# A RetNet block and a quick-GELU MLP on one core: a new order of loads, conversions and products up to the fifth unit

## The chip, the cores and the metric

The kernel runs on one core of one Trainium2 chip, as one launch. A core has five engines that work side by side, each through its own queue of instructions in order: PE (TensorE, matrix products; PEld is its loading of stationary operands), DVE (VectorE, elementwise), ACT (ScalarE, elementwise functions and copies), POOL (GpSimd, elementwise) and SP (SyncE, which here only issues DMAs). DMAs are issued by SP, ACT and POOL. The metric is the device time of one execution in microseconds (us), the median over runs.

## The reference, cut to what matters

Two parts, one after the other. `retnet_recurrent` keeps a 64 x 64 state for each of 4 batches and 8 heads over 768 positions:

```python
for t in range(S):                          # S = 768
    state = gamma[h] * state + outer(k[:, :, t], v[:, :, t])
    y[:, :, t] = scale * q[:, :, t] @ state
```

Its output, put together over the heads, is `x` with 3072 rows of 512. `act_gelu_quick` then computes

```python
h = x @ w_in                                # 512 -> 2048
g = h * (1 / (1 + exp(-1.702 * h)))
out = g @ w_out                             # 2048 -> 512
```

All inputs are float32 for q, k, v and 64-bit floats for `w_in` and `w_out`, which the kernel gets as pairs of 32-bit words and narrows itself to float32. The result is float32.

## The kernel before, in words

**Units.** The recurrence is done in chunks of 64 positions. A unit j is one chunk for two batches (batch on the two halves of the 128 partitions) and all eight heads. Units 0 to 11 are the first two batches. For a unit:

- `load(j)` fetches q (SP, four DMAs of 64 KB for j < 6), k (POOL, for unit 0 ACT, four DMAs) and v (SP, two DMAs of 128 KB). q and v have two buffers each, so unit j+2 loads into the buffer of unit j once that is done with.
- `turn(j)` transposes q and k on PE for j < 6: four 128 x 128 transposes each, into two PSUM tiles; `turned(j)` copies them to SBUF on ACT. From unit 6 on, the transposes are done on DVE (L253).
- `step{j}-{f}` is `attend(j, f)` on PE: for unit j the products k by q (L289, PSUM tile `pa`), and for an earlier unit f its state update k by v (L297), its share from the state (L306) and from the chunk itself (L312, PSUM tile `py`). `step{j}` is the first part alone, `step-{f}` the others alone. `pa` and `py` have one buffer each.
- `masked(j)` on DVE multiplies `pa` by a causal decay mask (L318). `decay(j)` on ACT scales k by its decay (L272, eight instructions). `aged(f)` on ACT scales the state (L357), `updated(f)` on DVE adds the new part (L366 for unit 0, a copy, and L368). `state{f}` (L325) and `x{f}` (L347, for unit 0 a copy on ACT, L349) on DVE put the output of the unit into X.

**Weights.** The weights come in sixteen pieces: w0 to w7 of `w_in`, w8 to w15 of `w_out`, each as two DMAs of 512 KB on SP ("a" and "b", L180) into one of three raw buffers (piece number modulo 3). Piece 0 is converted by halves, the others whole. A conversion is one ACT instruction, `abs` (L207), and six on DVE: `half` (L211, L212, L213) and `rest` (L217, L218, L222). A raw buffer is free for its next piece when `rest` is done.

**Products.** `up0.th.p` (L414, 16 matmul instructions of 256 columns) is the first MLP product for two units (th = 0: units 0 and 1, th = 1: units 2 and 3) with weight piece p; `gate` applies quick-GELU on ACT (L393). The first blocks of products are begun as soon as their units and weight pieces are there, between the steps of later units; from unit 8 on, the kernel runs in a regular order that this change does not touch.

**Start.** The mask is made from `rows` (a product on PE, L862), `mask` (DVE, L901) and `causal` (two instructions on POOL, L866). `rowd` (ACT, L872) reads `rows` too; `whole` (POOL, two small DMAs) loads the state's decay. `warm` is a matmul on PE whose result nobody reads. `table` loads ACT's function table.

**The order.** What each engine does until the regular part starts is written out by hand as one list of names, and carried out name by name. `pin` keeps an instruction in that order on its engine, and PE is wholly in program order. The relative order of two names matters only where they use the same engine or the same buffer. The change rewrites the first seven lines of that list.

Of the kernel before, what the change touches and what calls it, by code (L numbers as in the profile page):

```python
# [9 lines left out]
F32 = mybir.dt.float32  # L10
U32 = mybir.dt.uint32
AF = mybir.ActivationFunctionType
# [16 lines left out]
def kernel(  # L29
# [29 lines left out]
    pe, act, dve, pool, sp = nc.tensor, nc.scalar, nc.vector, nc.gpsimd, nc.sync  # L59
# [41 lines left out]
    rowd = const.tile([P, HP, D], F32, name="rowd")  # L101
# [3 lines left out]
    whole = const.tile([P, HP], F32, name="whole")  # L105
    whole_h = const.tile([P, H], F32, name="whole_h")
    ident = const.tile([P, P], F32, name="ident")
    mask = const.tile([P, 2, HP, D], F32, name="mask")
# [9 lines left out]
    def pin(i):  # L118
        return tc.keep_in_program_order(i) if ordered[0] else i
# [62 lines left out]
    class Narrow:  # L182
# [30 lines left out]
            pin(dve.scalar_tensor_tensor(hi, hi, 0x80000000, mu, op0=ALU.bitwise_and, op1=ALU.bitwise_or))  # L213

        def rest(self):
            m, mu, lo, hi = self.m, self.mu, self.lo, self.hi
            pin(dve.tensor_scalar(mu, hi, 0xFF800000, None, op0=ALU.bitwise_and))  # L217
            pin(dve.scalar_tensor_tensor(lo.bitcast(F32), lo, 2.0 ** -52, m, op0=ALU.mult, op1=ALU.mult))  # L218
            a, b = lo.bitcast(F32), hi.bitcast(F32)
            if self.i < NFF:  # L220
                a, b = [t.rearrange("p (c ab f) -> p c ab f", ab=2, f=P) for t in (a, b)]
            pin(dve.tensor_add(self.w, b, a))  # L222
# [8 lines left out]
    def home(j, name):  # L231

        at = ["qT", "kT", "kd", "at"].index(name)
        shape = [[HP, P] if j < NEW else [H, D]] * 2 + [[H, D], [2, HP, D]]
        shape = shape[at]
        if j >= 2 * CB:
            return one.tile([P] + shape, F32, name=name, tag=name, bufs=[2, 1, 1, 2][at])
        t = G[:, at, j % 2 * 2:j % 2 * 2 + 2].rearrange("p s t -> p (s t)")
        return t.rearrange("p (a b c) -> p a b c", a=2, b=HP) if at == 3 else t.rearrange("p (a b) -> p a b", a=shape[0])

    def turn(j):

        QT[j], KT[j] = home(j, "qT"), home(j, "kT")
        if j < NEW:

            x = QKV.pop(("q", j)), QKV["kn", j]
            TURNED[j] = p = [ps.tile([P, HP, P], F32, name="pt", tag="y") for i in range(2)]
            for n in (1, 0) if j else (0, 1):
                for s in range(HP):
                    pe.matmul(p[n][:, s, :], x[n][:, 2 * s:2 * s + 2].rearrange("p r d -> p (r d)"), ident, is_transpose=True)  # L250
        else:
            for t, name in ((QT[j], "q"), (KT[j], "k")):
                tc.keep_in_program_order(dve.transpose(  # L253
                    t.rearrange("p h t -> p (h t)"), QKV.pop((name, j)).rearrange("p h n d -> p (h n d)")))
        if 2 * CB <= j < NCH - 2:
            load(j + 2, "qk")

    def turned(j):
        p = TURNED.pop(j)
        for n in (1, 0) if j else (0, 1):  # L260
            pin(act.activation((QT[j], KT[j])[n], p[n], AF.Copy))

    def decay(j):
# [98 lines left out]
    def updated(f):  # L362
        c = f % NC
        new, u = state[(c + 1) % 2], PU.pop(f)
        if c == 0:
            pin(dve.tensor_copy(new, u))  # L366
        elif c < NC - 1:
            pin(dve.tensor_add(new, new, u))  # L368

    def step(j, f=None):  # L370
        attend(j, f)
        if j is not None:
            masked(j)
            if j > 2 * CB:
                decay(j)
        if f is not None:
            c = f % NC
            if c == 0:
                updated(f)
            else:  # L380
                by_state(f)
            output(f)
            if 0 < c < NC - 1:
                aged(f)
                updated(f)
        if j is not None and 2 * CB < j < NCH - 1:
            load(j + 1, "v")
# [255 lines left out]
    def down49(m, ring, comps):  # L643
# [25 lines left out]
        def home2(name, first, rest):  # L669
            kept[name] = first.rearrange("p (j e) -> p j e", e=P), rest[:, 0:3 * P].rearrange("p (j e) -> p j e", e=P)  # L670
            return kept[name]
# [169 lines left out]
    works, products = {}, {}  # L841
# [63 lines left out]
    for j in range(2 * CB):  # L905
        for name in "qkv":
            works[f"{name}{j}"] = lambda j=j, name=name: load(j, name)
        works |= {f"{name}{j}": lambda j=j, do=do: do(j) for name, do in (
            ("turn", turn), ("turned", turned), ("decay", decay), ("masked", masked), ("state", by_state),
            ("x", output), ("aged", aged), ("updated", updated))}  # L910
        for f in (None, *range(2 * CB)):
            works[f"step{j}" + ("" if f is None else f"-{f}")] = lambda j=j, f=f: attend(j, f)
        works[f"step-{j}"] = lambda j=j: attend(None, j)
# [7 lines left out]
        works[f"w{i // 2}{'ab'[i % 2]}"] = lambda i=i: fetch(i)  # L921
    for name, i in [("0a", 0), ("0b", 1)] + [(str(p), 2 * p) for p in range(1, NFF)]:
        n = Narrow(i)
        works |= {"abs" + name: n.start, "half" + name: n.half, "rest" + name: n.rest}

    units = [0]

# [14 lines left out]

    begin()
    for name in """
        k0 table q0 warm turn0 w0b rows warm k1 abs0b q1 turned0 step0 v0 w0a half0b mask k2 turn1 causal rest0b
        masked0 decay0 v1 decay1 abs0a half0a step-0 updated0 turned1 q2 step1 rowd whole w2b turn2 w2a x0 k3
        aged1 masked1 turned2 v2 rest0a abs2 q3 step-1 updated1 state1 decay2 aged2 step2 q4 x1 half2 decay3 w3b
        w3a up0.0.0 masked2 turn3 k4 step-2 v3 q5 rest2 k5 gate0.0.0 turned3 updated2 state2 step3 up0.0.2
        masked3 abs3 half3 x2 rest3 turn4 w1b step-3 aged3 gate0.0.2 turned4 state3 w1a w5b updated3 v5 decay4
        abs1 x3 turn5 half1 up0.0.3 turned5 up0.1.2 step4 aged4 w5a rest1 v4 gate0.0.3 decay5 w6a masked4  # L950
        gate0.1.2 abs5 w6b step5-4 half5 rest5 up0.0.1 updated4 abs6 state4 gate0.0.1 w4b
        up0.1.1 half6 aged5 w4a up0.0.5 rest6 masked5 up0.1.5 gate0.1.1 x4 gate0.0.5 abs4 step-5 w8b w8a
        half4 gate0.1.5 state5 updated5 anew q6 up0.1.6 x5 rest4 gate0.1.6 abs8 v6 decay6 aged6 up0.0.6 w7b w7a half8
        turn6 gate0.0.6 up0.1.0 abs7 seven_4.2 seven_6.2 half7 gate0.1.0 w9b w9a up0.1.4 q7 gate0.1.4 step6 masked6 rest7 up0.0.4 v7
        gate0.0.4 seven_52.2 turn7 up0.1.3 gate0.1.3 step7-6 seven_4.0 masked7 updated6 decay7 aged7 abs9 state6 x6 up0.0.7 rest8 seven_w.0 gate0.0.7
        w11a w11b step-7 state7 x7 seven_x half9 w10b w10a up0.1.7 gate0.1.7
        seven2.0 seven2.1 abs11 rest9 seven2.2 seven_v.0 w12a w12b seven2.3 half11 seven2.4 abs10 seven_4.1 seven_w.1
        seven2.5 rest11 seven2.6 w14b w14a seven0.0 seven0.1 half10 seven0.2 abs12 seven0.3 rest10 w13a w13b seven0.4
        seven_v.1 seven0.5 seven_4.3 half12 seven_w.3 seven0.6 seven1.0 abs14 seven1.1 rest12 w15a w15b seven1.2 seven1.3
        half14 seven1.4 abs13 seven_v.3 seven1.5 updated7 rest14 seven1.6 seven3.0 seven3.1 half13 seven3.2 abs15 seven3.3  # L960
        rest13 seven3.4 seven3.5 late_loads half15 rest15 seven3.6 seven_end
    """.split():
        works[name]()
    ordered[0] = False
    INNER = [(0, 19), (0, 22), (0, 26), (1, 2), (1, 12), (1, 15), (1, 18)]
    for m in range(NB):
        between = []
        if m == 0:
            between = [lambda: None, lambda: None, lambda: turn(2 * CB), lambda: step(2 * CB), lambda: None,
                       lambda: turn(2 * CB + 1)]  # L970
        elif m == 1:
            between = [lambda: (decay(2 * CB), load(2 * CB + 1, "v"))]
            for j in range(2 * CB + 1, 3 * CB + 1):
                between.append(lambda j=j: (step(j, j - 1), j < 3 * CB and turn(j + 1)))
        elif 1 < m < NB - 1:
            last = min((m + 2) * CB, NCH - 1)
            for j in range((m + 1) * CB + 1, last + 1):
                between.append(lambda j=j: (step(j, j - 1), j < last and turn(j + 1)))
            if last == NCH - 1:
                between.append(lambda: step(None, NCH - 1))  # L980
# [77 lines left out]
```

## Time and profile before

| | |
|---|---|
| median of 3 runs | 662.11 us (660.8 to 662.55) |
| the profiled execution: its own time | 662.24 us |
| its span, first to last instruction | 660.5 us |
| PE busy | 642.2 us, 97% of the span |
| DVE busy | 453.9 us, 69% |
| ACT busy | 159.0 us, 24% |
| POOL busy | 198.8 us, 30% |
| DMA | 91.86 MB, mean 139 GB/s |

The profile is one execution taken by the hardware profiler. Its page gives busy shares of engines, the same in 40 slices of the span (a digit is tenths; PEclk is the clock granted to TensorE), the chain of work that ended last, and the costliest groups of instructions by line. The timeline lists instructions in order of time: start, duration, engine, line, operation, operands, and in brackets the idle time before it with what ended that. A line number is that of the kernel as printed above. Instructions that only issue DMAs, wait or branch do not count as busy.

### The profile page before, as it was taken

How to read it: one execution, taken by the hardware profiler on the slowest of the kernel's cores; microseconds unless marked ns; L12 is line 12 of the kernel's file. 1: busy time of each engine (PE TensorE's matmuls, PEld its weight loads, DVE VectorE, ACT ScalarE, POOL GpSimd, SP SyncE). 2: the span in 40 equal slices, each digit the busy share in tenths (PEclk: the TensorE clock that was granted, in tenths of full speed). 3: DMA queues.
4: the chain of work that ended last, by engine and by line, in shares of the span. 5: the costliest groups of instructions: out<-in, count | busy, mean ns of one | idle time of the engine just before them, and what ended most of it. 6: DMA issues, size and time to landing. Idle time of an engine off the chain costs nothing.

```text
span 660.5 us, 15291 instructions
## 1 busy us (share of the span) xinstructions
PE 642.2 (97%) x6390; PEld 580.2 (88%) x6390; DVE 453.9 (69%) x645; ACT 159.0 (24%) x306; POOL 198.8 (30%) x225
## 2 busy tenths in 40 slices
PE   6789999999999999999999999999999999999997
PEld 3778888888788888889999888999888999988997
DVE  3699989999936973556984445995354995254965
ACT  4674233551000000333100233010233110233110
POOL 6400311310379217000536400445600255500000
PEclk9989999999999999999999999999999999999999
DMA  9995549763233556262485832386742252602142
GB/s 176 193 274 173 152 104 241 172 163 60 49 82 135 137 149 153 58 248 96 118 199 134 279 57 97 86 223 135 225 118 97 66 154 104 235 21 96 55 154 96
DMA packets 148149, 91.86 MB, mean 139 GB/s; under 512 B 131600, under 2 KB 134416, under 8 KB 147056
## 3 DMA queue, kind: packets, MB, share of 16 engines
q1 hardware_dynamic: 135856, 45.19, 29.8%
q0 software_dynamic: 9888, 44.46, 20.6%
q10 hardware_dynamic: 2336, 1.25, 0.6%
q8 instruction: 50, 0.82, 0.5%
q14 instruction: 19, 0.16, 0.1%
HBM read 72.89 MB, written 15.47 MB: 134 GB/s over the span
## 4 chain that ended last, share of the span: by engine, by line
PE 89%; DVE 4%; DMA 4%; SPq 1%; issue 1%; ACT 0%; DVEq 0%
PE pq L666 27%; PE px L562 17%; PE pd L799 13%; PE py L562 13%; PE ph L491 7%; PE ph L414 5%; PE pa L289 2%; PE py L312 2%; PE pa L297 2%; PE py L306 2%; DMA W<-in_moe_w_in_dram 1%; DMA W<-in_moe_w_out_dram 1%; DMA q_in<-in_q_dram 1%; PE pt L250 1%; SPq L140 1%
## 5 line engine op out<-in xcount | busy, mean ns | idle before, releaser
L635 POOL DMA_DIRECT2D ring<-W2D x28 | 15.4, 551 | 227.7 <-PE px L562 118.3
L666 PE MATMUL pq<-W,G 128*128 128x128 f32 x672 | 80.2, 276 | 0.0
L666 PEld LDWEIGHTS pq<-W,G 128*128 128x128 f32 x672 | 77.6, 192 | 1.3 <-issue 0.7
L666 PE MATMUL pq<-ring,own 128*128 128x128 f32 x448 | 60.1, 276 | 1.3 <-issue 1.3
L562 PE MATMUL px<-X,W1A 128*128 128x256 f32 x256 | 59.8, 379 | 0.0
L562 PE MATMUL px<-X,W1B 128*128 128x256 f32 x256 | 59.8, 379 | 0.0
L666 PEld LDWEIGHTS pq<-ring,own 128*128 128x128 f32 x448 | 54.5, 192 | 0.4
L562 PEld LDWEIGHTS px<-X,W1B 128*128 128x128 f32 x256 | 48.5, 190 | 6.7
L562 PEld LDWEIGHTS px<-X,W1A 128*128 128x128 f32 x256 | 48.4, 190 | 6.5
L393 ACT ACTIVATE G<-G 128x512 f32<-128x512 f32 x60 | 37.4, 628 | 54.7 <-DVE G L572 33.4
L799 PE MATMUL pd<-W,G 128*128 128x256 f32 x224 | 49.6, 381 | 0.0
L799 PEld LDWEIGHTS pd<-W,G 128*128 128x128 f32 x224 | 42.2, 190 | 5.9
L562 PE MATMUL py<-X,W1A 128*128 128x256 f32 x192 | 45.4, 379 | 0.0
L562 PE MATMUL py<-X,W1B 128*128 128x256 f32 x192 | 45.4, 379 | 0.0
L562 PEld LDWEIGHTS py<-X,W1A 128*128 128x128 f32 x192 | 36.5, 190 | 5.0
L562 PEld LDWEIGHTS py<-X,W1B 128*128 128x128 f32 x192 | 36.5, 190 | 5.0
L580 DVE TENSOR_TENSOR t<-py,u 128x512 f32<-128x512 f32 x16 | 11.1, 692 | 32.3 <-PE py L562 32.3
L569 ACT ACTIVATE p<-px 128x512 f32<-128x512 f32 x16 | 9.6, 597 | 96.0 <-PE px L562 96.0
L414 PE MATMUL ph<-X,W1A 128*128 128x256 f32 x128 | 30.6, 397 | 0.9 <-DVE X L347 0.9
L594 DVE TENSOR_TENSOR G<-G 128x512 f32<-128x512 f32 (+2 forms) x24 | 12.3, 513 | 25.7 <-ACT G L393 25.7
L666 PE MATMUL pq<-ring,G 128*128 128x128 f32 x224 | 29.6, 275 | 0.0
L666 PE MATMUL pq<-W,own 128*128 128x128 f32 x224 | 29.6, 275 | 0.0
(237 smaller groups left out, 1226.0 us busy)
## 6 DMA issues: line engine op xcount, KB each, us to landing
ring<-W2D POOLq DMA_DIRECT2D x28, 768.0 KB, 4.8
W1B<-W1D POOLq DMA_DIRECT2D x6, 1792.0 KB, 9.8
W<-in_moe_w_in_dram SPq DMA_DIRECT2D x12, 512.0 KB, 5.9
W<-in_moe_w_out_dram SPq DMA_DIRECT2D x10, 512.0 KB, 5.8
out_dram<-o POOLq DMA_DIRECT2D x20, 256.0 KB, 3.0
q_sq<-in_q_dram SPq DMA_DIRECT2D x144, 32.0 KB, 2.1
k_sq<-in_k_dram SPq DMA_DIRECT2D x144, 32.0 KB, 2.1
v_in<-in_v_dram SPq DMA_DIRECT2D x72, 64.0 KB, 3.1
```

Source lines behind the costliest of these rows:

```text
L289: pe.matmul(pa[HALF[w], u, 0, s, :], kt[HALF[u], w, s, :], qt[HALF[u], w, s, :], start=True, stop=True)
L297: pe.matmul(pa[HALF[u], w, 1, s, :], kd[HALF[w], HP * u + s, :], vn[HALF[w], HP * u + s, :], start=True, stop=True)
L306: pe.matmul(py[HALF[o], u, 1, 2 * w + s2, :], old[HALF[u], w, 2 * s2 + o, :], qt[HALF[u], w, 2 * s2 + o, :], start=True, stop=True)
L312: pe.matmul(py[HALF[o], w, 0, 2 * u + s2 if f < NEW else 2 * s2 + u, :], vn[HALF[w], HP * u + s, :], a[HALF[w], u, s, :], start=True, stop ...
L393: pin(act.activation(g, h[:, i], AF.Gelu_apprx_sigmoid))
L414: pe.matmul(h[:, ab], w, X[:, 2 * th + c // 2, c % 2, :], start=(ab == 0 and c == 0), stop=(c == 3), skip_group_check=True)
L491: pe.matmul(acc[:, u, :], w, x, start=(start and u == 0 and c == 0), stop=(stop and c == 1), skip_group_check=True)
L562: pe.matmul(acc[:, u, :], t[:, q1 + u, sa, c, :], X[:, sb, c, :], start=(start and u == 0 and c == 0), stop=(stop and c == 1), skip_group_ ...
L594: dve.tensor_sub(q[0][1], q[0][0], q[0][1])
L635: pool.dma_start(c, W2D[i])
L666: pe.matmul(p0[:, j, :], a[:, d], w[:, d], start=(new and j == 0 and d == 0), stop=(d == NP // 2 - 1), skip_group_check=True)
L799: pe.matmul(p0[:, n, :], g1(m, p, sa)[:, n * P:(n + 1) * P], W2[:, sb, p, :], start=(new and p == 0 and n == 0), stop=(last and p == NP - ...
```

## The change

- The order of names up to unit 5 is new. On SP both halves of w0 are now issued first, ahead of q0 and v0; then w2 ahead of q1 and v1; w3 ahead of q2; w1 ahead of v3 and q4; w5 ahead of v4 and q5.
- On POOL, `causal` and `whole` now stand ahead of the loads of k2.
- `rest` is split into `resta` (two instructions) and `restb` (one), which can stand apart; for pieces 2, 3 and 1 other DVE work now stands between them.
- `turn0` transposes k first and then q, as the other units do; `turned0` likewise.
- `updated0`, a copy of the first state out of PSUM, is done on ACT and no longer on DVE.
- `step2` stands behind the first product and not ahead of it; `step3-2` is one step for units 3 and 2. `turn5` and `turned5` stand behind `step4`, and `abs5` behind `turned5`.

```diff
         def rest(self):
+            self.resta()
+            self.restb()
+
+        def resta(self):
             m, mu, lo, hi = self.m, self.mu, self.lo, self.hi
             pin(dve.tensor_scalar(mu, hi, 0xFF800000, None, op0=ALU.bitwise_and))
             pin(dve.scalar_tensor_tensor(lo.bitcast(F32), lo, 2.0 ** -52, m, op0=ALU.mult, op1=ALU.mult))
-            a, b = lo.bitcast(F32), hi.bitcast(F32)
+
+        def restb(self):
+            a, b = self.lo.bitcast(F32), self.hi.bitcast(F32)
             if self.i < NFF:
                 a, b = [t.rearrange("p (c ab f) -> p c ab f", ab=2, f=P) for t in (a, b)]
             pin(dve.tensor_add(self.w, b, a))
...
-            for n in (1, 0) if j else (0, 1):
+            for n in (1, 0):
...
-        for n in (1, 0) if j else (0, 1):
+        for n in (1, 0):
             pin(act.activation((QT[j], KT[j])[n], p[n], AF.Copy))
...
-        if c == 0:
+        if f == 0:
+            pin(act.activation(new, u, AF.Copy))
+        elif c == 0:
             pin(dve.tensor_copy(new, u))
...
-        works |= {"abs" + name: n.start, "half" + name: n.half, "rest" + name: n.rest}
+        works |= {"abs" + name: n.start, "half" + name: n.half, "rest" + name: n.rest,
+                  "resta" + name: n.resta, "restb" + name: n.restb}
...
-        k0 table q0 warm turn0 w0b rows warm k1 abs0b q1 turned0 step0 v0 w0a half0b mask k2 turn1 causal rest0b
-        masked0 decay0 v1 decay1 abs0a half0a step-0 updated0 turned1 q2 step1 rowd whole w2b turn2 w2a x0 k3
-        aged1 masked1 turned2 v2 rest0a abs2 q3 step-1 updated1 state1 decay2 aged2 step2 q4 x1 half2 decay3 w3b
-        w3a up0.0.0 masked2 turn3 k4 step-2 v3 q5 rest2 k5 gate0.0.0 turned3 updated2 state2 step3 up0.0.2
-        masked3 abs3 half3 x2 rest3 turn4 w1b step-3 aged3 gate0.0.2 turned4 state3 w1a w5b updated3 v5 decay4
-        abs1 x3 turn5 half1 up0.0.3 turned5 up0.1.2 step4 aged4 w5a rest1 v4 gate0.0.3 decay5 w6a masked4
-        gate0.1.2 abs5 w6b step5-4 half5 rest5 up0.0.1 updated4 abs6 state4 gate0.0.1 w4b
+        w0b w0a k0 table q0 v0 warm abs0b w2b w2a k1 abs0a half0b turn0 q1 rest0b rows turned0 step0 v1 half0a mask warm
+        decay0 causal whole w3b rest0a w3a k2 masked0 abs2 step-0 decay1 updated0 k3 turn1 half2 turned1 q2 step1 x0 rowd
+        resta2 masked1 restb2 aged1 step-1 v2 abs3 state1 x1 updated1 turn2 q3 up0.0.0 turned2 w1b w1a decay2 half3 step2
+        gate0.0.0 k4 resta3 masked2 v3 aged2 turn3 restb3 turned3 up0.0.2 q4 abs1 decay3 step3-2 gate0.0.2 masked3 state2
+        x2 updated2 half1 up0.0.3 k5 w5b w5a aged3 resta1 step-3 v4 gate0.0.3 state3 x3 updated3 turn4 q5 turned4 restb1
+        up0.1.2 decay4 step4 aged4 v5 w6a turn5 masked4 turned5 abs5 up0.0.1 gate0.1.2 decay5 w6b
+        step5-4 half5 rest5 updated4 abs6 state4 gate0.0.1 w4b
         up0.1.1 half6 aged5 w4a up0.0.5 rest6 masked5 up0.1.5 gate0.1.1 x4 gate0.0.5 abs4 step-5 w8b w8a
```

## The prediction

> **What bounds the kernel now.** I read the page first. TensorE is busy 642.2 us, 97% of the 660.5 us span; only the first slices of the span, where this change is made, show an engine under 9 tenths.
>
> ```profile
> PE   6789999999999999999999999999999999999997
> ...
> DVE  3699989999936973556984445995354995254965
> ...
> PEclk9989999999999999999999999999999999999999
> ```
>
> From about 56 us on PE hardly waits, so a gain must come out of the first 56 us and must then survive what follows. The timeline of PE has the gaps (last bracket: idle time and who ended it).
>
> ```profile
> 16.15 1.14 PE L297 MATMUL pa<-v_in,G 64*64 64x64 f32 x32 [0.49 <-issue]
> ...
> 20.75 1.13 PE L289 MATMUL pa<-G 64*64 64x64 f32 x32 [2.62 <-DVE state L366]
> ...
> 28.09 3.72 PE L414 MATMUL ph<-X,W1A 128*128 128x256 f32 x16 [0.94 <-DVE X L347]
> ...
> 36.07 0.69 PE L289 MATMUL pa<-G 64*64 64x64 f32 x32 [1.83 <-DVE state L368]
> ...
> 45.39 7.07 PE L414 MATMUL ph<-X,W1A 128*128 128x256 f32 x32
> ...
> 94.13 0.69 PE L289 MATMUL pa<-G 64*64 64x64 f32 x32 [0.72 <-DVE G L253]
> ```
>
> Two more things show in it. Until about 26.5 us the same work takes nearly double (32 small matmuls 1.13 us, later 0.69). And the first gap of 1.83 us is followed by a slow product. The table by stage says why: the granted clock was halved.
>
> ```profile
> 33.50:37.00 3.50, 1.67 (x85) 1.49 (x78) 3.17 (x5) 2.64 (x6) 0.00 (x0) 0.99 1.21 293
> 37.00:40.40 3.40, 3.40 (x9) 2.70 (x8) 3.33 (x5) 1.51 (x5) 0.00 (x0) 0.50 0.88 226
> ...
> 54.20:71.70 17.50, 17.50 (x289) 15.43 (x283) 16.44 (x19) 5.92 (x12) 0.40 (x1) 1.00 0.54 150
> ```
>
> (PE, PEld, DVE, ACT, POOL busy; clock; DMA share; GB/s.) The third row: DVE is busy 16.44 of 17.50 us, so it is nearly as full as PE there. The chain of work that ended last runs through it:
>
> ```profile
> 71.73 0.69 DVE tmp L325
> ...
> 76.76 0.40 SPq L180
> ...
> 78.23 8.88 DMA W<-in_moe_w_out_dram
> ...
> 93.27 0.72 DVE G L253
> 94.13 0.69 PE pa L289 x32
> ```
>
> PE waits 0.72 us at 94.13 for this: last lines of a weight conversion on DVE (to 76.74), four weight DMAs on SP, unit 7's q and k queued behind them, DVE's transposes, then PE. PE arriving earlier at 94 gains nothing; what sets the end is when DVE and SP arrive at 76.8.
>
> **What the Trainium skill says.** "TensorE: Matmul & The Clock Gate", Part 1: the clock is halved after an idle window of about 3.4 us that runs free of the program, and is restored after a busy one. The trace agrees in size: 3.4 us at 0.50, starting in a stretch where PE was busy 1.67 of 3.5 us. So a gap near 1.8 us may or may not cost it, by where the window lies. The same page, "Architectural detail": ACT's and DVE's queues are strictly first in, first out; the timeline agrees. "DMA: Bandwidth & Descriptors", "Issuing engines are not separate DMA queues": all DMAs share the same engines. "Anatomy of one DMA": a wait is made by the issuing sequencer, so what is behind it on SP waits too; the trace has v1's first DMA on SP held to 10.07, when the first weight piece lands (10.06).
>
> **The change, part by part.** *Weights first.* SP issues w0b, w0a (512 KB each), then q0's four DMAs. The SP and ACT issues of before fit a rule of eight in flight: the ninth (w0b, 4.18) waits for the landing of the first (k0, 4.17), v1 (the 17th) for w0b's, w2a (the 24th, 17.59) for w0a's (17.57). In the new order, w0b, w0a, k0 x4, q0 x4, q0's third DMA waits for w0b to land and its fourth for w0a. Landing of w0a: k0's first DMA takes 3.4 us (0.81 to 4.17); another 1.25 MB at 300 GB/s (between 157 of the first 10 us and 390 where weights are alone) is 4.2; so about 8.4 us. Bounds: 6.9 (1 MB at 390, k0 hidden) and 9.8 (w0a took 8.98 in before). Then q0's last DMA, 3.7 us to landing as before: 12.1, not 6.6.
>
> What is late next: rows stands behind turn0 on PE. Half a turn 0.99: 13.1; rows 2.07: 15.2; mask 0.68: 15.9; causal on POOL 1.85: 17.8; masked0 0.68 and 0.1 to pass on: step-0 at 18.6, before 16.15. The second warm (2.08) and step0 (1.13) lie beside it. Then step-0 1.99, turn1 1.97, its last copy 0.7, step1 at 23.3 (before 20.75). Moving updated0 from DVE (0.68) to ACT (one PSUM copy, 0.60) and halves of the conversion no longer ahead of it remove the 2.62 gap, leaving 0.7. Then step1 1.13, masked1 0.84, step-1 2.84, turn2 between 1.03 and 1.97: first product at 29.6, before 28.09. Lost: 1.5 us. The order k before q of turn0 costs nothing: k0 has landed while q0 is awaited. k2 behind causal and whole, and q2 behind w3a (which waits for rest0a on DVE), have until about 28; I take them as hidden, with 2 us or less to spare.
>
> *The middle.* Now w2 is converted ahead (resta2, restb2 around masked1; before, it ended at 35.3), so the 1.83 gap and its halved clock (5.41 against 3.62 us for 16 matmuls: 1.8) go. Product 3.46, step2 0.66, turn3 1.03, product 3.46, step3-2 0.66 and 1.64: 40.5. From here PE needs up0.0.3 3.46, step-3 1.6, turn4 1.03, and stands at 46.6 before up0.1.2. That needs x3, and DVE has in order state2, x2, updated2 (0.6 each), half1 2.7, resta1 1.95, state3 0.6, x3 0.69: 7.8, so 48.4. A new gap of 1.8 us, the size of the one removed. Product to 51.9 (before 52.46).
>
> *abs5 behind turned5.* Before, abs5 followed gate0.1.2 (53.05). Now it stands on ACT behind turned5, so behind step4 0.66, turn5 1.03 and the copy 0.66: 54.3; half5 after its 1.15: 55.4, before 54.20. DVE is 1.2 late although PE is 0.2 early (up0.1.1: 51.9 + 0.66 + 1.03 + 3.46 + 2.26 = 59.3, before 59.5).
>
> *From there.* rest5, then w8 and unit 6's loads on SP, which issue without rest from 60.16 to 76.33, with 0.43 to spare before w7. So w7 comes 1.2 - 0.43 = 0.8 late; DVE alone would have 1.2 less its 0.68 wait at 71.73. At 94.13 PE then stands 0.8 later and waits about 1.7. Sum without any halved clock: 660.5 + 0.8 = 661.3; the execution's own time is 662.24, 1.74 more, which makes 663.0. That execution lies 0.13 above the median of 662.11. Each of the two gaps of 1.7 to 1.8 us can halve the clock for 1.8 us. I put each at a half, since the one gap of this size that the trace has did it. One of two is likeliest: 664.8; both 666.6; none 663.0.
>
> **Rivals.** *Faster: the first weights land early.* Place: q0's fourth DMA. If w0a lands at 6.9 rather than 8.4 and q0 then needs 2.6 rather than 3.7, the chain to 29.6 runs 2.6 earlier, DVE reaches half5 before 54.2, and the 1.83 gap with its slow clock is gone for good: 663.0 - 2.6 = 660.4, or 660 if the clock also recovers earlier. It decides at q0 landing before about 10. For it: 390 GB/s where weights run alone. Against: k0, and k1 on POOL, run beside it. *No change: hidden.* If SP, not abs5, decides at 76.8 and w8's lateness is taken up in SP's loads, PE's wait at 94 grows from 0.72 but the end stays: 662.1. For it: 0.43 to spare; against: 1.2 exceeds it. *Slower still: q2 or k2 late at turn2.* POOL's k loads issued between 16 and 23 us took 5.3 to 7.8 us to land; each us past 28 is a us on PE, and gives 666 to 667. *The change not doing what it says:* weights do come first on SP, but the conversion is then held by the mask (rows) on DVE, so half of the gain of early weights is not used; this is in the sum.
>
> **How the numbers follow.** One halved clock 0.40 (664.8), both or q2/k2 late 0.15 (666.6), none 0.20 (663.0), hidden 0.10 (662.1), faster 0.15 (660). A measurement of this kernel tells about 0.3%, or 2 us: slower is above 664.1, faster below 660.1. So slower 0.55, same 0.30, faster 0.15. Range 659.8 to 667.2; that of the slower cases alone is 663.5 to 667.2.
>
> **What would show it.** Right: q0's third and fourth DMA issued on SP only at the landings of w0b and w0a; the q half of turn0 and rows on PE after 11 us; step1 after 22; no wait at the step after the first product; a PE gap of 1.5 to 2 us before up0.1.2, ended by DVE's X line 347; half5 after 54.8; PE's wait at step7-6 above 1 us; a clock of 0.50 after one of these gaps. Wrong: q0 landing by 10, half5 before 54.2, or DVE ahead of PE through 76 us. Then the end moves with DVE, and it is faster.

## The result and the profile after

The changed kernel takes 664.78 us, the median of 8 runs (661.25 to 665.51), beside 661.87 us for the kernel before (8 runs, 657.44 to 663.03): a ratio of 1.0049, with an interval of 1.0026 to 1.0073. It was measured again in two further sessions, each on one chip, beside 56 and 62 runs of the kernel before: 1.0023 [1.0001, 1.0045] and 1.0035 [1.0020, 1.0050]. It is slower by some 0.2 to 0.5%. The profiled execution took 663.73 us and has a span of 662.0 us, 1.5 us more than the one before, where the medians differ by 2.9: single executions of one kernel lie up to 8 us apart.

The page of the kernel after, busy tenths in 40 slices of 16.6 us:

```profile
PE   4789989999999999999999999999999999999997
...
DVE  3877979999936874556984445995254995254965
...
PEclk9999989999999999999999999999999999999999
```

PE's first slice fell from 6 to 4 tenths; DVE's slice two rose from 6 to 8, and its slices three and four fell from 9 to 7. The conversions now start early, and DVE rests later. The slice with a lower clock is the sixth here and was the third before. PE's timeline (start, duration, engine, line, operands, in brackets the idle time before it and what ended it):

```profile
11.85 1.09 PE L256 MATMUL pt<-ident,q_in 128*128 128x128 f32 x4 [0.76 <-DMA q_in<-in_q_dram]
12.86 2.07 PE L870 MATMUL rows<-G 1*128 1x512 f32 x2
...
18.82 1.13 PE L303 MATMUL pa<-v_in,G 64*64 64x64 f32 x32 [0.82 <-ACT W1A L207]
...
23.39 0.69 PE L295 MATMUL pa<-G 64*64 64x64 f32 x32 [0.69 <-ACT G L267]
...
27.59 0.63 PE L256 MATMUL pt<-ident,kn_in 128*128 128x128 f32 x4 [1.06 <-DMA kn_in<-in_k_dram]
...
28.49 3.62 PE L422 MATMUL ph<-X,W1A 128*128 128x256 f32 x16
...
47.38 3.69 PE L422 MATMUL ph<-X,W1A 128*128 128x256 f32 x16 [1.90 <-DVE X L353]
...
86.80 5.41 PE L422 MATMUL ph<-X,W1B 128*128 128x256 f32 x16 [1.85 <-ACT X L401]
92.04 3.62 PE L422 MATMUL ph<-X,W1A 128*128 128x256 f32 x16
95.59 0.69 PE L295 MATMUL pa<-G 64*64 64x64 f32 x32
```

Up to step1 the early part is late by what was forecast (23.39, before 20.75), the first product by only 0.4 us (28.49, before 28.09). The old gap of 1.83 us near 36 us is gone, and 1.90 us stand ahead of up0.1.2 (47.38). The gap before 86.80 is new, and the product behind it takes 5.41 us instead of 3.6. The table by stage (PE, PEld, DVE, ACT, POOL busy; clock; DMA share; GB/s) shows the halved clock there, and DVE still nearly full in the middle (16.84 of 17.50 us):

```profile
54.20:71.70 17.50, 17.50 (x289) 15.18 (x288) 16.84 (x20) 8.39 (x23) 1.61 (x2) 1.00 0.37 91
87.60:91.10 3.50, 3.50 (x10) 2.75 (x9) 3.43 (x5) 0.00 (x0) 0.00 (x0) 0.51 0.27 42
```

From step7-6 on the two executions take the same time: 662.0 less 95.59 is 566.4, and 660.5 less 94.13 is 566.4. So the 1.5 us lie before it, and the chain of work that ended last (start, duration, what) tells who brings them:

```profile
76.80 0.78 DVE W L212
77.58 0.42 SPq L180
...
78.03 6.94 DMA W<-in_moe_w_in_dram
...
85.08 1.12 ACT W1B L207
86.20 0.27 ACT W1A L401
86.47 0.28 ACT X L401
...
86.80 8.86 PE ph L422 x32
```

Piece w7 comes late, abs7 on ACT waits for it, gate0.1.0 stands behind abs7 on ACT, and the next product stands behind that gate. Where the last of the head start of the conversions went is seen on DVE's timeline:

```profile
6.04 0.46 DVE L211 TENSOR_SCALAR W1A<-W1A 128x512 f32<-128x512 f32 x1 [4.97 <-ACT W1A L207]
...
51.76 0.69 DVE L324 TENSOR_TENSOR G<-pa,mask 128x512 f32<-128x512 f32 x1 [2.80 <-PE pa L295]
54.45 0.69 DVE L211 TENSOR_SCALAR W1B<-W1B 128x1024 f32<-128x1024 f32 x1 [2.00 <-ACT W1B L207]
```

The start of each conversion on DVE (`half`, L211), in us; the last two columns are kernels E6 and E11 below:

| piece | before | after | E6 | E11 |
|---|---|---|---|---|
| w0b | 10.78 | 6.04 | 6.01 | 11.49 |
| w2 | 28.92 | 18.64 | 18.70 | 19.57 |
| w3 | 37.43 | 28.59 | 30.29 | 29.95 |
| w1 | 46.67 | 41.24 | 42.68 | 43.51 |
| w5 | 54.20 | 54.45 | 51.01 | 51.84 |
| w7 | 83.79 | 86.23 | 82.80 | 83.62 |

The change puts the conversions up to 10.3 us ahead (w2). The lead is 8.8 us at w3 and 5.4 at w1, and nothing is left of it at w5 (0.25 us behind), where DVE idles 2.80 and 2.00 us: for PE's step4, and for abs5, which ACT has only behind turned5. So about half of the lead goes before abs5 comes into play, and the rest at w5.

### The profile page after: what moved, and what is told of

It is laid out like the page before. It is cut to its first block, busy times and chain, and to the rows that moved or that the text cites. A ratio compares the mean times of both kernels' runs of the same rounds, so it can differ in the third digit from the quotient of the medians.

```text
span 662.0 us, 15290 instructions
## 1 busy us (share of the span) xinstructions
PE 640.1 (97%) x6390; PEld 576.9 (87%) x6390; DVE 451.6 (68%) x644; ACT 159.6 (24%) x307; POOL 200.4 (30%) x225
## 4 chain that ended last, share of the span: by engine, by line
PE 84%; DVE 7%; DMA 4%; POOL 2%; issue 1%; ACT 1%; SPq 0%; DVEq 0%; POOLq 0%; ACTq 0%
PE pq L674 25%; PE px L570 16%; PE pd L807 13%; PE py L570 12%; PE ph L499 7%; PE ph L422 4%; DMA kn_in<-in_k_dram 3%; PE pa L295 2%; PE py L318 1%; PE py L312 1%; PE pa L303 1%; DMA W<-in_moe_w_in_dram 1%; DMA q_in<-in_q_dram 1%; PE pt L256 1%; DVE W L222 1%
## 5 line engine op out<-in xcount | busy, mean ns | idle before, releaser
L570 PEld LDWEIGHTS px<-X,W1A 128*128 128x128 f32 x256 | 48.2, 190 | 7.3 <-POOL X L540 0.9
L422 PE MATMUL ph<-X,W1B 128*128 128x256 f32 x128 | 30.7, 398 | 1.8 <-ACT X L401 1.8
L422 PE MATMUL ph<-X,W1A 128*128 128x256 f32 x128 | 29.2, 381 | 1.9 <-DVE X L353 1.9
L422 PEld LDWEIGHTS ph<-X,W1B 128*128 128x128 f32 x128 | 25.1, 199 | 5.8 <-ACT X L401 2.0
```

Of the source, the lines that this page charges most:

```text
L422: pe.matmul(h[:, ab], w, X[:, 2 * th + c // 2, c % 2, :], start=(ab == 0 and c == 0), stop=(c == 3), skip_group_check=True)
L570: pe.matmul(acc[:, u, :], t[:, q1 + u, sa, c, :], X[:, sb, c, :], start=(start and u == 0 and c == 0), stop=(stop and c == 1), skip_group_ ...
```

## The experiments

The theory: abs5's place on ACT makes half5, then w7's DMA, late, and that sets PE's start of step7-6. The rivals: the late q0 costs it; the new gap before up0.1.2 costs it; the halved clock costs it; w7's slow landing costs it. E1 to E4 ran on one chip, E5 to E8 on a second, E9 to E12 on a third. The changed kernel itself ran on the second and third only (E5, E12), so E1 to E3 have no changed kernel beside them.

**E1.** abs5 ahead of turn5's copy, the rest as changed.

```diff
-        up0.1.2 decay4 step4 aged4 v5 w6a turn5 masked4 turned5 abs5 up0.0.1 gate0.1.2 decay5 w6b
+        up0.1.2 decay4 step4 aged4 abs5 v5 w6a turn5 masked4 turned5 up0.0.1 gate0.1.2 decay5 w6b
```

> The changed kernel with abs5 on ACT ahead of turned5 (behind aged4) instead of behind it; nothing else. My theory: half5 on DVE then starts right behind masked4, at 52.4 instead of 54.45 us, and w7's DMAs are issued about 1.2 to 2 us sooner (76.2 or before instead of 77.44); PE's gap of 1.85 us at 86.8 and the halved clock behind it shrink or go: 2 to 3.6 us less than the changed kernel, so 661 to 662.8 us, about the kernel before. Rival, the loss is set in the first 30 us by the late q0: DVE moves but the end does not, 664 to 665. Rival, w7's slow landing (6.2 to 6.9 us against 4.0 to 5.3) is what makes the gap: 664 too, with the gap still there.

Measured 660.16 us, 0.9998 [0.9983, 1.0013]. half5 starts 4.99 us after up0.1.2 instead of 7.07. But in this execution up0.1.2 itself came only at 49.05, so half5 stands at 54.04 and w7 is issued at 77.09, not at the 52.4 and 76.2 that were expected. There is no gap at 86, as there is none in E5 and E12 without this move. The median speaks for the theory; this profile alone doesn't show it.

**E2.** resta1, two DVE instructions, behind x3.

```diff
-        x2 updated2 half1 up0.0.3 k5 w5b w5a aged3 resta1 step-3 v4 gate0.0.3 state3 x3 updated3 turn4 q5 turned4 restb1
+        x2 updated2 half1 up0.0.3 k5 w5b w5a aged3 step-3 v4 gate0.0.3 state3 x3 updated3 resta1 turn4 q5 turned4 restb1
```

> The changed kernel with resta1 on DVE behind updated3 instead of ahead of state3; nothing else. My theory: state3 and x3 come at once after step-3, the gap of 1.90 us before up0.1.2 becomes at most 0.6, up0.1.2 starts near 46.0 instead of 47.38, and abs5, half5 and w7's issue move with it by 1 to 1.4 us: 662 to 663.5. Rival, PE's lead is lost again at 94 us as it was in the kernel before: 664 to 665. Rival, w1 comes too late for up0.0.1 and the gap moves there: no gain or 0.5 us.

Measured 659.96 us, 1.0006 [0.9989, 1.0023]. On PE's timeline of E2 the gap fell from 1.90 to 0.61, so x3's place on DVE makes it, as the prediction has it:

```profile
48.08 3.69 PE L422 MATMUL ph<-X,W1A 128*128 128x256 f32 x16 [0.61 <-DVE X L353]
```

PE waits 1.64 us at step7-6 (94.67), about what the unaltered kernel waits there in E5 (1.82).

**E3.** gate0.1.0 ahead of abs7 on ACT.

```diff
-        turn6 gate0.0.6 up0.1.0 abs7 seven_4.2 seven_6.2 half7 gate0.1.0 w9b w9a up0.1.4 q7 gate0.1.4 step6 masked6 rest7 up0.0.4 v7
+        turn6 gate0.0.6 up0.1.0 gate0.1.0 abs7 seven_4.2 seven_6.2 half7 w9b w9a up0.1.4 q7 gate0.1.4 step6 masked6 rest7 up0.0.4 v7
```

> The changed kernel with gate0.1.0 on ACT ahead of abs7; nothing else. My theory: the gap of 1.85 us at 86.8 is PE waiting for the PSUM buffer that gate0.1.0 frees, and that gate stands on ACT behind abs7, which waits for w7 to land. With the gate ahead the gap goes, and PE then waits before step7-6 for unit 7's transposes, near 94 to 95 us, for 1.5 to 2 us instead. Gain at most 1.8 us where the halved clock goes, 0 to 0.5 where it comes there: 662.5 to 664.5. Rival, the end is set by PE and the PSUM wait alone: 3 us or more less, 661.5.

Measured 660.39 us, 1.0012 [0.9991, 1.0033]. The gap at 86 can't arise now; PE waits 1.73 us at step7-6. E1 to E3 each come out level with the kernel before. They act on one chain, ahead of abs5, at abs5 and behind w7, so what they bring need not add up; and the changed kernel on that chip is missing. They show the waits and what ends them; how much each is worth they don't settle.

**E4.** k0 and q0 first again, w0 behind them, abs0b behind turned0.

```diff
-        w0b w0a k0 table q0 v0 warm abs0b w2b w2a k1 abs0a half0b turn0 q1 rest0b rows turned0 step0 v1 half0a mask warm
+        k0 table q0 w0b w0a v0 warm turn0 turned0 abs0b w2b w2a k1 abs0a half0b q1 rest0b rows step0 v1 half0a mask warm
```

> The changed kernel with q0 ahead of w0 on SP again, and turned0 ahead of abs0b and abs0a on ACT; nothing else. My theory: turn0 runs by 8 us instead of 12.9, but mask on DVE stands behind half0a, which now waits for w0 to land (10 to 11.5 us), so mask starts near 13.5 instead of 14.97; step-0 at 17.3 instead of 18.8, and turn2 still waits for k2, which starts when causal is done, 1.4 us earlier. The first product starts 1 to 1.4 us sooner, and the end comes 0.5 to 1.4 us sooner: 663.3 to 664.3. Rival, the early order is what costs the whole loss: 662 or less. Rival, hidden: 664.8.

Measured 662.38 us, 1.0036 [1.0019, 1.0054]: not faster. turn0 runs at 6.57, but the mask is behind half0a on DVE and comes later (15.63) than in the changed kernel (14.97), so what PE had gained was lost at step-0. PE's timeline of E4:

```profile
19.47 1.13 PE L303 MATMUL pa<-v_in,G 64*64 64x64 f32 x32 [5.89 <-DVE G L324]
```

Later half5 is at 55.42, w7 is issued at 78.26, and PE waits 2.48 and 1.36 us at 88.39 and 96.92. Of the four kernels on this chip it is the one that has abs5, resta1 and gate0.1.0 where the changed kernel has them, and the only one that is slower than the kernel before; but its start differs too.

**E5.** The changed kernel, unaltered.

> The changed kernel as it is, on the chip of the other experiments, as their base. If the loss is the kernel's and not the chip's: 1.003 to 1.007 of the kernel before. PE's gap near 86.8 ended by ACT, with the waits of abs7 and gate0.1.0 ahead of it, or in a run whose clock came late no gap there and 1.6 us before step7-6 at 94.

Measured 662.04 us, 1.0023 [1.0001, 1.0045]. Its profile has no halved clock and no gap at 86: w7's halves landed in 4.6 us here, and in 6.2 and 6.9 in the first profile. PE's timeline has the wait at step7-6, where the prediction put it:

```profile
93.76 0.69 PE L295 MATMUL pa<-G 64*64 64x64 f32 x32 [1.82 <-DVE G L259]
```

**E6.** The changed kernel with DVE's conversions kept ahead: abs5 and half5 before step4, resta1 as in E2, gate0.1.0 as in E3.

```diff
-        up0.1.2 decay4 step4 aged4 v5 w6a turn5 masked4 turned5 abs5 up0.0.1 gate0.1.2 decay5 w6b
-        step5-4 half5 rest5 updated4 abs6 state4 gate0.0.1 w4b
+        up0.1.2 decay4 abs5 half5 step4 aged4 v5 w6a turn5 masked4 turned5 up0.0.1 gate0.1.2 decay5 w6b
+        step5-4 rest5 updated4 abs6 state4 gate0.0.1 w4b
```

> The changed kernel with four moves at once: abs5 and half5 ahead of step4 and masked4, where DVE is idle for 2.8 us; resta1 behind x3; gate0.1.0 ahead of abs7. My theory: w5 is converted 4 us sooner, w6, w4 and w7's issue are then bound by PE's step-5 and by SP, the gap before up0.1.2 is 0.6 us, the one at 86.8 is gone and the wait before step7-6 under 0.7: 5 to 7 us less than the changed kernel, 3 to 4 less than the one before (0.994 to 0.996 of it). Rival, the loss lies before the first product: 1.000 to 1.003. Rival, PE has no more than its 0.7 us to gain at 94 us: 0.998 to 1.000.

Measured 659.13 us, 0.9982 [0.9966, 0.9997], beside 1.0023 for E5 on the same chip: 659.13 / 662.04, or 0.44% less. It beats the changed kernel (the two intervals don't overlap) and, narrowly, the kernel before (the interval ends at 0.9997). The size is that of the second rival in the expectation, not of the theory. DVE's and PE's timelines of E6:

```profile
51.01 0.69 DVE L211 TENSOR_SCALAR W1B<-W1B 128x1024 f32<-128x1024 f32 x1
```

```profile
92.13 0.69 PE L295 MATMUL pa<-G 64*64 64x64 f32 x32
```

No wait is left on PE at either place. Here PE itself decides at 92, so the rest of DVE's lead buys nothing there: of the 3.2 us by which half5 is earlier than before (54.20), w7's issue keeps 1.2 (75.57, before 76.76).

**E7.** The kernel before with nothing but w0 first.

```diff
-        k0 table q0 warm turn0 w0b rows warm k1 abs0b q1 turned0 step0 v0 w0a half0b mask k2 turn1 causal rest0b
+        w0b w0a k0 table q0 warm turn0 rows warm k1 abs0b q1 turned0 step0 v0 half0b mask k2 turn1 causal rest0b
```

> The kernel before with w0b and w0a on SP ahead of k0 and q0, nothing else: the first part of the change alone. My theory: q0 lands near 11.8 us instead of 6.6, rows and mask come 2.7 us later, step-0 at 18.8 instead of 16.15; updated0 no longer waits for w0a (17.57), so step1 at 21.6 to 22.0 instead of 20.75; the first product 0.5 to 1.3 us later, and by up0.1.1 nothing to 1 us is left: 1.000 to 1.002 of the kernel before. Rival, the late q0 costs the whole loss: 1.004 to 1.006. Rival, early weights are a gain: 0.997.

Measured 660.4 us, 1.0003 [0.9983, 1.0023]. PE's timeline of E7:

```profile
11.86 1.08 PE L250 MATMUL pt<-ident,q_in 128*128 128x128 f32 x4 [5.88 <-DMA q_in<-in_q_dram]
```

q0 is as late as in the changed kernel and step-0 later (20.69), yet the median does not move. So putting w0 first, with the late q0 that it brings, does not cost the loss. E7 can't say whether the late q0 costs something that the early w0 gives back: in its profile, of the fastest of its 14 runs, half5 starts at 52.03, 2.2 us earlier than before.

**E8.** k2 ahead of causal on POOL, because of the 1.06 us wait at 27.59.

```diff
-        decay0 causal whole w3b rest0a w3a k2 masked0 abs2 step-0 decay1 updated0 k3 turn1 half2 turned1 q2 step1 x0 rowd
+        decay0 k2 causal whole w3b rest0a w3a masked0 abs2 step-0 decay1 updated0 k3 turn1 half2 turned1 q2 step1 x0 rowd
```

> The changed kernel with k2's loads on POOL ahead of causal and whole instead of behind them; nothing else. In the changed kernel turn2 waits 1.06 us for k2. My theory: the first product starts 0.4 to 1 us sooner (q2 lands only 0.5 us before k2), and 0.3 to 1 us of that is left at the end: 1.002 to 1.004 of the kernel before. Rival, k2's packets now hold up w2, q1 and v1, which abs2 and turn1 need: same as the changed kernel or slower. Rival, hidden by the waits at 87 to 95 us: same.

Measured 662.56 us, 1.0044 [1.0029, 1.0058], no better than E5. The wait for k2 is gone, and PE waits 1.20 and 1.26 us before step1 and step-1 (0.69 and 0.81 in the changed kernel). The first product starts at 28.56; but in this execution the clock was halved from 25.2 to 28.6, over step-1 and turn2, so the profile doesn't say where it would start otherwise.

**E9.** The changed kernel with abs5 later still, behind gate0.1.2 and decay5.

```diff
-        up0.1.2 decay4 step4 aged4 v5 w6a turn5 masked4 turned5 abs5 up0.0.1 gate0.1.2 decay5 w6b
+        up0.1.2 decay4 step4 aged4 v5 w6a turn5 masked4 turned5 up0.0.1 gate0.1.2 decay5 abs5 w6b
```

> The changed kernel with abs5 moved 2.65 us further back on ACT, behind gate0.1.2 and decay5; nothing else: a larger dose of the suspected cost. My theory: half5 starts at 57 instead of 54.4, rest5, masked5, w7's issue and PE's step7-6 all come about 2.6 us later, and so does the end: 1.006 to 1.008 of the kernel before, PE waiting 3 to 4 us in the stretch from 85 to 96 us. Rival, the place of abs5 doesn't matter and the loss comes from the start: as the changed kernel, 1.002 to 1.005.

Measured 665.22 us, 1.0081 [1.0051, 1.0110], beside 1.0035 for E12 on the same chip. DVE's timeline of E9:

```profile
58.28 0.69 DVE L211 TENSOR_SCALAR W1B<-W1B 128x1024 f32<-128x1024 f32 x1 [4.44 <-ACT W1B L207]
```

half5 waits 2.4 us longer for abs5 than in the changed kernel, and the median grows by 2.4 us (665.22 less 662.8). Nothing else was altered, so abs5's place does cost time. The way is not quite the expected one: of the 3 to 4 us of waiting expected from 85 to 96 us there are 1.33 (96.83), and PE waits already for w5 itself, for the last line of its conversion:

```profile
64.36 7.14 PE L422 MATMUL ph<-X,W1B 128*128 128x256 f32 x32 [1.12 <-DVE W1B L228]
```

The profiles of the unaltered kernel have no such wait there.

**E10.** The kernel before, given the suspected cause alone: abs6 ahead of abs5 on ACT.

```diff
-        gate0.1.2 abs5 w6b step5-4 half5 rest5 up0.0.1 updated4 abs6 state4 gate0.0.1 w4b
+        w6b gate0.1.2 abs6 abs5 step5-4 half5 rest5 up0.0.1 updated4 state4 gate0.0.1 w4b
```

> The kernel before with abs6 ahead of abs5 on ACT, so that half5 starts 1.15 us later (55.35 instead of 54.20), with w6b's DMA ahead of both; nothing else: the suspected cost put into the kernel before. My theory: w7's issue and PE's step7-6 come 0.7 to 0.8 us later, the wait of 0.72 us there grows to 1.5: 1.001 of the kernel before, no gain in any case. Rival, a slack of SP or DVE takes it up: 1.000.

Measured 662.99 us, 1.0041 [1.0024, 1.0059]. DVE's and PE's timelines of E10:

```profile
55.74 0.69 DVE L211 TENSOR_SCALAR W1B<-W1B 128x1024 f32<-128x1024 f32 x1 [2.61 <-ACT W1B L207]
```

```profile
86.35 3.72 PE L414 MATMUL ph<-X,W1B 128*128 128x256 f32 x16 [0.60 <-ACT X L393]
...
94.88 0.69 PE L289 MATMUL pa<-G 64*64 64x64 f32 x32 [1.35 <-DVE G L253]
```

One abs put ahead of abs5 makes the kernel before as slow as the changed one, with waits at both places (none at 86 and 0.72 us at 94 in its own profile). This was expected at 1.001; the loss is larger. The delay is larger too, as ACT's timeline of E10 shows:

```profile
53.49 1.20 ACT L207 ACTIVATE W1B<-W 128x1024 f32<-128x1024 f32 x1 [1.05 <-DMA W<-in_moe_w_in_dram]
54.57 1.14 ACT L207 ACTIVATE W1B<-G 128x1024 f32<-128x1024 f32 x1
```

abs6 waits 1.05 us for w6 to land, and abs5 waits behind it. abs5 starts 2.5 us after the second half of gate0.1.2 (52.06), in the kernel before 0.3 (52.78 to 53.05): 2.2 us lost, not the 1.15 of one abs.

**E11.** E6 with k0 and q0 first, and turned0, decay0 and the mask ahead of the conversions.

```diff
-        w0b w0a k0 table q0 v0 warm abs0b w2b w2a k1 abs0a half0b turn0 q1 rest0b rows turned0 step0 v1 half0a mask warm
-        decay0 causal whole w3b rest0a w3a k2 masked0 abs2 step-0 decay1 updated0 k3 turn1 half2 turned1 q2 step1 x0 rowd
+        k0 table q0 w0b w0a v0 warm turn0 turned0 rows decay0 abs0b w2b w2a k1 mask step0 q1 abs0a causal half0b warm v1
+        whole masked0 k2 rest0b w3b half0a rest0a w3a abs2 step-0 decay1 updated0 k3 turn1 half2 turned1 q2 step1 x0 rowd
```

> The version with DVE ahead (four moves), and besides q0 ahead of w0 on SP, turned0 and decay0 ahead of abs0b on ACT, mask ahead of half0b on DVE, k2 ahead of rest0b. My theory: rows and mask are done by 11.5 us, masked0 by 13.5, step-0 near 14 to 15 instead of 18.9; turn1 then waits for q1 (17 to 18 us), and step1 comes at 20 to 21 instead of 23.4; the first product near 26.5 to 27.5 instead of 28.5 to 29.8. Since nothing waits at 94 us in the version with DVE ahead, what is gained stays: 0.994 to 0.997 of the kernel before. Rival, w2 and w3 come later and DVE gives it back: 0.998.

Measured 662.2 us, 1.0019 [1.0002, 1.0036]: worse than E6's ratio, and far from the 0.994 to 0.997 expected. PE's timeline of E11:

```profile
14.34 1.14 PE L303 MATMUL pa<-v_in,G 64*64 64x64 f32 x32 [0.90 <-DVE G L324]
...
20.76 1.13 PE L295 MATMUL pa<-G 64*64 64x64 f32 x32 [2.07 <-ACT G L267]
25.05 1.13 PE L303 MATMUL pa<-v_in,G 64*64 64x64 f32 x32 [3.16 <-DVE G L324]
...
30.30 0.63 PE L256 MATMUL pt<-ident,q_in 128*128 128x128 f32 x4 [1.36 <-DMA q_in<-in_q_dram]
```

Step-0 is 4.5 us earlier than in E6 (18.87), and all of it is lost again by 30 us, to turned1, masked1 and q2. The conversions, meanwhile, start 5.5 us later (11.49) and stay 0.8 us behind E6 from w1 to w7 (table above). w7 is issued 0.8 us later (76.39), and PE waits 0.74 us at step7-6 (93.76). PE's early gain was worth nothing. That DVE's late start is the cost fits these times, but E11 alters several things at once, and only E6 on another chip stands beside it.

**E12.** The changed kernel, unaltered, on the third chip.

> The changed kernel once more, as the base of these three on their chip: 1.002 to 1.005 of the kernel before. If the loss is what PE waits at 85 to 96 us: w7 issued near 76.6 to 77.4, and PE waits 1.8 us there in a run without a halved clock.

Measured 662.8 us, 1.0035 [1.0020, 1.0050]. A wait of 1.37 us at step7-6 (93.14), no halved clock.

**Together.** In twelve of the fourteen profiles w7 is issued 22.0 to 23.1 us after half5, whatever the kernel: before 54.20 and 76.76, after 54.45 and 77.44, E9 58.28 and 80.39, E10 55.74 and 78.17. In E6 and E11, where DVE is far ahead and waits for PE in between, it is 24.6.

So it is shown that a later abs5 makes the kernel slower (E9, and E10 in the kernel before), and that with the conversions kept ahead it is faster (E6, four moves at once). That abs5's place is the whole loss against the kernel before is not shown. half5 stands at 54.45, 54.35 and 54.19 in the three profiles of the changed kernel and at 54.20 in that of the kernel before; in E5 and E12 w7 is issued at 76.60 and 76.56 (before 76.76) and step7-6 starts at 93.76 and 93.14 (before 94.13). The loss of their medians is not seen in these two profiles at all, and the kernel before was profiled only once, in another session. w7's landing, 3.6 to 8.6 us for one half over the profiles, was not tested apart.

## Why the prediction was right, and where not

- **Direction: right. Size: right by luck.** 664.8 us was forecast and 664.78 measured; the later two ratios would be some 1.5 to 2.3 us more than the kernel before. The forecast has 1.8 us of halved clock in it, which six of the eight runs don't have, and the median of these six is 664.78 too. For a run without it the sum gave 663.0.
- **"abs5 behind turned5": right in the step, not in its size against the kernel before.** abs5 was forecast at 54.3, that is 5.9 us after up0.1.2 (48.4), and half5 7.0 after it. Measured 53.28 and 54.45, which is 5.9 and 7.07 after 47.38. E9 and E10 show that the end follows a delay of abs5. The absolute times were 1.0 late (see the clock below), and with that the delay against the kernel before is 0.25 us at half5, where 1.2 was forecast.
- **"A new gap of 1.8 us" before up0.1.2: right** (1.90, ended by DVE's X line); E2 shows its cause. The terms of that sum give 48.2 for up0.1.2, not the 48.4 written there, which changes nothing.
- **q0 late: right in size, wrong in mechanism.** q half of turn0 was forecast at 12.1 (11.85), rows at 13.1 (12.86), step-0 at 18.6 (18.82), step1 at 23.3 (23.39). But q0's third DMA was not held until w0b had landed (5.33), and its fourth not until w0a had (7.28). They were issued at 5.84 and 6.49; the third was held for k0's first piece, which landed only at 5.83, as SP's waits up to 12 us in the kernel after show (what waited for what: us in total, times, longest):

```profile
SPq L140 <- DMA kn_in<-in_k_dram: 3.5, 2, 2.5
```

  They then took 5.3 to 5.6 us to land, not 3.7, side by side with w0 and k1. Two errors cancelled. The Trainium skill ("DMA: Bandwidth & Descriptors", "Issuing engines are not separate DMA queues") says that all issuers' DMAs run on the same engines and interleave; these landings fit that, and the sum had used a landing time from a stretch without such company.
- **"First product at 29.6": 28.49.** The term is the granted clock, taken as released at 26.5, where the kernel before had it; here it was at 22.8, and 32 small matmuls took 0.69 us instead of 1.13 from step1 on. The forecast of k2 as "hidden" was off by 1.06 us, which this covered.
- **"SP has 0.43 spare, w7 0.8 late": right in size in one profile, wrong in the step.** A delay of 1.2 us at half5 was to shrink by 0.43; it was 0.25 and grew to 0.68 at w7's issue, and in E5 and E12 w7 is not late. What followed was mis-sized: w7's halves needed 6.2 and 6.9 us to land, before 4.0, and abs7 on ACT began 2.5 us later (85.08 against 82.58). So most of the 1.5 us that this profile loses up to step7-6 comes in behind w7's issue, with the landing and the halved clock. That a late w7 stops PE through gate0.1.0 behind abs7, ahead of step7-6, was not foreseen. E5 and E12 have the wait at step7-6 alone that the prediction describes (1.82 and 1.37 us, forecast 1.7), but at 93.76 and 93.14, not at the forecast 94.9.
- **"Each of the two gaps halves the clock with chance a half": wrong.** The mean granted clock tells whether a run had a drop of this kind (0.997 or less, otherwise 0.999 or more), though not where. The changed kernel had one in 2 of 8, 3 of 12 and 2 of 22 runs, the kernel before in 149 of 169. The profiled one had it, though not at 36 or 48 us but at 87. So the likeliest case of the prediction is not what most runs of the changed kernel are.
- **Sum without it, "+0.8": too small.** The three sessions gave 2.9, 1.5 and 2.6 us; runs of the changed kernel without a drop alone give 2.9, 0.6 and 2.4. E10 shows how much a late abs5 can cost: 0.41%, 2.7 us on a median of 660.24, for 2.2 us of delay. The gain that was set against the loss, the end of the halved clock at 36 us, seems to be worth nothing: in the kernel before, runs with a drop have medians of 659.7, 660.4 and 660.3 us in the three later sessions, and those without 660.7, 660.9 and 660.0. E7, with no drop in 14 runs where the kernel before has 50 in 56, has the same time too. Why is not shown; PE may wait for DVE later anyway, but the profile of E7 reaches step7-6 at 91.15 without a wait. In the changed kernel a drop went with a longer time in E5 (medians of 663.09 with one and 661.13 without) and E12 (664.0 and 662.6), not in the first session (664.5 and 664.8); these are seven runs with a drop in all.

Of the rivals, "first weights land early" is out: q0 landed at 11.8, and step-0 came late. "Hidden" is out as a rule with E9 and E10, where a later half5 does reach the end. "q2 or k2 late" occurred for 1.06 us, and E8 shows that taking it away brings nothing. Still open: how the loss of the changed kernel splits, and how the 2.7 us of E10 do. E10's single profile shows 0.75 us at step7-6 against a profile of the kernel before from another session, and single executions differ by more than that. Open too is what E6's lead in DVE could yet give if PE were faster up to 92 us.

## What to carry to other kernels

Find the queue that really sets a stage's end (here DVE's conversions, whose end lets SP fetch the next weights) and follow its start times from piece to piece: a head start of 10 us had shrunk to 5.4 two pieces later, and the rest was lost at one instruction placed too far back on another engine's in-order queue. Before giving that queue a wait, see what is behind it and who fetches on its completion. Time that PE gains or loses ahead of such a point need not be a gain or a loss of the kernel (E4, E7, E11).

## What was not expected of the hardware

- With the same order of work at the start, the clock was released at 22.8 (after), 30.4 (E1), 30.8 (E2), 17.9 (E3), 22.4 (E5), 28.1 (E6), 30.0 (E9) and 22.1 us (E12). The first product moves with it (27.61 in E3, 28.49 after, 30.14 in E2). A single profile of the start says little to 2 us.
- The length of a gap does not decide whether the clock is halved: not after 1.90 us (after, E1), 1.82 (E5) or 2.48 (E4), but after 1.83 (before) and 1.85 (after), and in E8 after gaps of 1.20 and 1.26. It stays halved for 3.4 us in these three. In the 3.4 us ahead of it PE was busy for less than half of the time (before 1.63 of 3.46 us, after 1.56 of 3.41, E8 1.45 of 3.41); whether that share decides was not tested. The free-running window of about 3.4 us of the Trainium skill ("TensorE: Matmul & The Clock Gate", Part 1) fits the duration, and that like gaps end differently; but the page speaks of an idle window, and in these runs gaps shorter than one were enough.
- The same code behind step7-6 takes 564.4 to 565.0 us in E1 to E4, 563.7 to 566.3 in E5 to E8 and 566.7 to 567.8 in E9 to E12. One wait makes a part of this: between 97 and 200 us PE idles 1.2 to 1.3 us in the profiles of E5, E6 and E8 to E12 (ended, as the profiles have it, by a line of DVE: L556, in E10 L548) and 0.04 or less in E1 to E4 and E7. Whether the chip or the single execution decides this is not known. Spans of single profiles can't be compared below 3 us.
